# The opening of a fused retention and feed-forward kernel in another order on ScalarE, GpSimd, VectorE and the sync engine

## The chip, the core and the metric

The kernel runs on one core of a Trainium2 chip (trn2). A core has five engines, each with an instruction queue of its own that it works off in order: TensorE (PE) for matrix products, VectorE (DVE), ScalarE (ACT) and GpSimd (POOL) for element-wise work, and the sync engine (SP), which here only issues DMAs and passes semaphores on. The metric is the device time of one execution in microseconds (us), as the median of several runs.

## What is computed

Retention (a causal, decaying form of attention without softmax) over 4 batches, 8 heads, 576 positions and head size 64, then two feed-forward layers on 2304 tokens of width 512. Cut to what matters:

```python
def _attn_ref(q, k, v):
    scores = scale * np.matmul(q, k.transpose(0, 1, 3, 2))
    gamma = 1.0 - 2.0 ** (-5.0 - np.arange(H))
    Dmat = np.where(rel >= 0, gamma[:, None, None] ** rel[None], 0.0)
    return np.matmul(scores * Dmat[None], v)

def _moe_ref(x, w_in, w_out):              # 512 -> 2048 -> 512, ELU
    h = x @ w_in
    g = np.where(h > 0.0, h, np.exp(np.minimum(h, 0.0)) - 1.0)
    return g @ w_out

def _moe2_ref(x, w_gate, w_val, w_out):    # 512 -> 1536 -> 512, gated
    gate = 1.0 / (1.0 + np.exp(-(x @ w_gate)))
    return gate * (x @ w_val) @ w_out
```

## The kernel before

**Retention in steps.** The 2304 tokens are worked off in 18 steps of 128 tokens (class `Step`). A step has a chunk of q, k and v (1 MB, one DMA; the last step of each half of the batches has six smaller ones, `load`, L172 to L187). Its methods are: `scale` (POOL multiplies v by powers of gamma, L192), `scores` (32 small matmuls into the PSUM tile `ts`, L197), `causal` (VectorE masks them into `a`, L207), `sums` (32 matmuls of k and v into the low half of the PSUM tile `to`, L210), `states` (VectorE adds them to the running state in two operations, L228 or L230 and L232, then POOL scales it, L233), `inter` (state times q into the high half of `to`, L238), `outs` (masked scores times v, onto the same place, L250), `x_scaled` (VectorE takes the result out of `to`, L267; ScalarE rounds it to its high half, L272) and `x_low` (VectorE forms the low half, L275). `inter` and `outs` use different row tiles of TensorE, and `inter` of its first half is fenced off by a relay: a no-op on another engine waits for it, and `outs` waits for the no-op (`swept`, L248 and L259). For steps 0 to 5 (`RELAY = 6`) the no-op is in ScalarE's queue, after that in SP's.

**Feed-forward in pieces.** Every product runs as three passes over high and low halves (`mm3`, L85). The first pass over the weights is cut in pieces of 256 tokens (`FF` with `half`): pieces 0 and 1 take the tokens of steps 0 and 1 with the weights `weights[0]` and `weights[2]` (two column blocks of w_in), pieces 2 and 3 the tokens of steps 2 and 3, and so on. `ups` of a piece is 12 matmuls (L291), in the order high x high, high x low, low x high, then ScalarE's Relu and Exp (L306, L307), VectorE's combination (L310) and a split into g's high half (ScalarE, L82) and low half (POOL, L83). `downs` of a piece follow `LAG = 2` pieces later with `weights[1]` and `weights[3]` (blocks of w_out).

**Weights.** They are stored as 64-bit floats. `Weight.chain` (L114) turns one into two float32 halves in five stages: two conversions on ScalarE (L121, L122), two operations on VectorE (L124, L125), one (L128), one (L130), then the split, high half on ScalarE (L82) and low half on POOL (L83). It is a generator: each `next` (`stage()`) puts the next stage into the queues.

**The order is written by hand** (`manual_schedule`): each engine works in the order of the program text. `block(n)` (L429) interleaves step n and step n+1 on TensorE: inter(n), scores(n+1), outs(n), sums(n+1). The opening (L454 to L464) is warm-up matmuls (`WARM`), block(-1), block(0), block(1) without its next step, with four stages of `weights[0]` inside block(1), and then the loop over pieces s (L486). In it, before the change, `weights[2]` is converted during piece 0, `weights[1]` during pieces 1 and 2, `weights[3]` during pieces 2 and 3; steps 2 and 3 begin only behind the ups of piece 1 (L500 to L507), then block(2) and block(3); piece 2 follows with block(4) behind its ups, piece 3 with block(5). Loads of later steps are issued on SP at fixed blocks (`loads_at`): load 5 in block(0), 6 in block(1), and so on; load 8 is the one of six DMAs, in block(3).

Below, x(n) is the high half of the result of step n, and a name like sums(4) means that method of step 4.

Of the kernel before, what the change touches and what calls it, by code (L numbers as in the profile page):

```python
# [28 lines left out]
NSTEP = (B // 2) * NS  # L29
# [5 lines left out]
N0 = 256  # L35
AHEAD = 2
LATE = 4
RELAY = 6
SPARE = {3: 2, 8: 2, 4: 3, 9: 3, 14: 3}
LAG = 2  # L40
WARM = 24, 6, 2, 10
# [7 lines left out]
def retention_elu_glu(  # L49
# [13 lines left out]
    pe, act, dve, pool, sp = nc.tensor, nc.scalar, nc.vector, nc.gpsimd, nc.sync  # L63
# [27 lines left out]
    def warm_up(n):  # L91

        h = h_bank()
        for i in range(n):
            pe.matmul(h[:, :256], warm[:, :128], warm, start=True, stop=True)

    def after(ins, other):

        tc.add_manual_dep(ins.ins, other.ins.name, mybir.DependencyInfo(
            mybir.DependencyClass.Sync, mybir.DependencyReason.DATA), reason="row tiles")  # L100
        return ins
# [4 lines left out]
    class Weight:  # L106
# [3 lines left out]
        def load(self, raw=None):  # L110
            self.raw = rpool.tile([128, 2 * DM], I32, tag="raw", name="raw") if raw is None else raw
            sp.dma_start(out=self.raw, in_=self.src.bitcast(I32))
# [29 lines left out]
    W, weights, of_pass = {}, [], []  # L142
# [12 lines left out]
    class Step:  # L155
# [82 lines left out]
        def inter(self):  # L238

            for other in (1, 0):  # L240
                for p in range(NP):
                    for h in range(2):
                        X, r = h ^ other, slice(64 * h, 64 * h + 64)
                        if X or self.c:
                            ins = self.mm(self.o(h, X, p), self.st[X][r, p, :], self.q[r, p, HC * X : HC * X + HC], p == 0)
                if other:

                    self.swept = after((act if self.n < RELAY else sp).nop(), ins)  # L248

        def outs(self):  # L250

# [127 lines left out]
    with tc.manual_schedule():  # L379
# [19 lines left out]
        steps = [Step(n) for n in range(NSTEP)]  # L399
# [25 lines left out]
        loads_at = {}  # L425
        for m in range(5, NSTEP):
            loads_at.setdefault(m - 5 if m < 13 or m == 14 else m - 3 if m == 13 else m - 4, []).append(steps[m].load)

        def block(n, after_it=True, mid=(lambda: None,) * 2):  # L429

            after_it = after_it and n + 1 < NSTEP
            if n >= 0:
                steps[n].inter()
                mid[0]()
            if after_it:
                steps[n + 1].scores()
            if n >= 0:
                steps[n].outs()
            if after_it:
                steps[n + 1].sums(n < 0)  # L440
                steps[n + 1].causal()
            for load in loads_at.get(n, []):
                load()
            if n >= 0:
                steps[n].x_scaled()
            mid[1]()
            if after_it:
                steps[n + 1].states()
                if 2 <= n < NSTEP - 2:
                    steps[n + 2].scale()  # L450
            if n >= 0:
                steps[n].x_low()

        warm_up(WARM[0])  # L454
        steps[0].scale()
        block(-1)
        warm_up(WARM[1])
        steps[1].scale()
        block(0)
        warm_up(WARM[2])  # L460
        first = weights[0].chain()
        block(1, False, (lambda: (next(first), next(first)), lambda: (next(first), next(first))))
        next(first)
        warm_up(WARM[3])  # L464


# [4 lines left out]
                ff += [FF(kind, P if kind == "a" else P - FA // FP, g, f, fs) for g in range(NG) for f in fs]  # L471
                begins.append(len(ff))

        conv = {0: weights[2], 1: weights[1], 2: weights[3]}
        for P in range(len(passes) - 1):
            a, b, ws = begins[P], begins[P + 1], of_pass[P + 1]
            a += 6 * (P == 0) + LAG * (P == 1)
# [8 lines left out]
        for s in range(len(ff) + LAG):  # L486
            chain = conv[s].chain() if s in conv else None
            stage = lambda: next(chain) if chain is not None else None
            stage()
            if halves is not None:  # L490
                next(halves)
            halves = chain
            if LATE <= s < NSTEP - AHEAD:
                block(s + AHEAD)
            if s < len(ff):
                ff[s].ups(stage, s)
            else:
                stage()
                stage()
            if s == 1:  # L500
                steps[2].scale()
                steps[2].scores()
                steps[2].sums(True)
                steps[2].causal()
                steps[2].states()
                steps[3].scale()
                block(2)  # L507
            if 0 < s < LATE:
                block(s + AHEAD)
            for w in loads.get(s, []):  # L510
                w.load()
            if s >= LAG:
                ff[s - LAG].downs(stage)
            else:
                stage()
            if s == begins[1] + LAG - 1:
                ret.close()
                wpools.append(ctx.enter_context(tc.tile_pool(name="w2", bufs=4, side="right")))
                psum["acc"] = ctx.enter_context(tc.tile_pool(name="ps_acc", bufs=4, space=bass.MemoryType.PSUM))
                ps_t = ctx.enter_context(tc.tile_pool(name="ps_t", bufs=1, space=bass.MemoryType.PSUM))  # L520
                tv = ps_t.tile([128, 2, 512], F32, name="tv")
# [50 lines left out]
def build(nc, arrays):  # L572
    args = [
        nc.dram_tensor(f"in_{n}", a.shape, mybir.dt.from_np(a.dtype), kind="ExternalInput").ap()
        for n, a in arrays.items()
    ]
    args.append(nc.dram_tensor("out_0", (NT, DM), F32, kind="ExternalOutput").ap())
    with tile.TileContext(nc) as tc:
        retention_elu_glu(tc, *args)
# [12 lines left out]
```

## Time and profile before

| | |
|---|---|
| median of 3 runs | 943.82 us (940.94 to 944.57) |
| the profiled execution | 942.38 us |
| its span, first to last instruction | 940.6 us |
| TensorE busy in the span | 910.4 us (97%), 6418 matmuls |
| VectorE, ScalarE, GpSimd busy | 467.8, 365.2, 304.4 us |
| mean granted TensorE clock | 0.989 of full speed |

The profile's row of the granted clock in 40 slices of 23.5 us is 9 (90% or more) nearly everywhere; its second slice, 23.5 to 47 us, is 6. The idle time of TensorE lies almost wholly in the first three slices.

### The profile page before, as it was taken

The page shows a single profiled execution, that of the slowest core. Times are in us where ns is not written, and L with a number is a line of the kernel's source. Part 1 is how long each engine was busy: PE and PEld are TensorE (multiplying, and loading weights), DVE is VectorE, ACT ScalarE, POOL GpSimd, SP SyncE. Part 2 cuts the span into 40 slices and gives each one's busy share as a digit, 9 for nine tenths or more (in the row PEclk, how much of TensorE's full clock was granted, in tenths as well). Part 3 has the DMA queues.
Part 4 walks back from the last instruction along what each step waited for, and adds up shares of the span by engine and source line. Part 5 has one row for each costly group of instructions (what it writes and reads, how often), then busy time and mean ns, then how long its engine had stood idle before and what let it go on. Part 6 is the DMA issues. An engine that isn't in the chain of part 4 may idle for free.

```text
span 940.6 us, 15386 instructions
## 1 busy us (share of the span) xinstructions
PE 910.4 (97%) x6418; PEld 770.9 (82%) x6418; DVE 467.8 (50%) x756; ACT 365.2 (39%) x673; POOL 304.4 (32%) x264
## 2 busy tenths in 40 slices
PE   6589899999999999999999999999999999999998
PEld 5579898888888888888888888888888888888886
DVE  3476644555554655546786333534344455343223
ACT  2135465544554444544674333222223223222111
POOL 2364433333333332333664222222132222222111
PEclk9699999999999999999999999999999999999999
DMA  9365521111111011111211111111011011100113
GB/s 344 130 191 166 156 68 32 59 45 45 45 46 45 25 57 32 46 45 45 68 46 51 40 45 45 45 46 45 23 57 56 22 46 48 43 23 1 46 45 113
DMA packets 26998, 60.55 MB, mean 64 GB/s; under 512 B 6576, under 2 KB 7600, under 8 KB 26928
## 3 DMA queue, kind: packets, MB, share of 16 engines
q1 hardware_dynamic: 24864, 56.89, 19.1%
q10 hardware_dynamic: 2064, 2.67, 0.8%
q8 instruction: 50, 0.82, 0.4%
q14 instruction: 20, 0.16, 0.1%
HBM read 54.84 MB, written 4.72 MB: 63 GB/s over the span
## 4 chain that ended last, share of the span: by engine, by line
PE 94%; DVE 2%; ACT 1%; DMA 1%; POOL 1%; issue 1%; ACTq 0%; DVEq 0%; POOLq 0%
PE acc L87 12%; PE acc L88 12%; PE acc L89 12%; PE h L87 11%; PE h L89 11%; PE h L88 11%; PE tv L88 5%; PE tv L87 5%; PE tv L89 5%; PE to L195 4%; PE h L291 2%; PE ts L195 1%; DMA vt<-in_csmall 1%; DVE e L267 0%; POOL w L83 0%
## 5 line engine op out<-in xcount | busy, mean ns | idle before, releaser
L83 POOL TENSOR_TENSOR g<-e,g 128x512 fp32r<-128x512 f32 (+1 forms) x148 | 167.1, 1129 | 567.6 <-ACT g L82 528.0
L87 PE MATMUL h<-x,w 128*128 128x512 f32 (+1 forms) x520 | 192.5, 370 | 0.0
L88 PE MATMUL h<-x,w 128*128 128x512 f32 (+1 forms) x520 | 192.3, 370 | 0.0
L89 PE MATMUL h<-x,w 128*128 128x512 f32 (+1 forms) x520 | 192.3, 370 | 0.0
L82 ACT CAST g<-e 128x512 fp32r<-128x512 f32 (+1 forms) x148 | 82.5, 557 | 232.0 <-DVE e L318 154.8
L318 DVE TENSOR_TENSOR e<-e,tv 128x512 f32<-128x512 f32 (+1 forms) x60 | 38.0, 634 | 231.8 <-PE tv L89 231.8
L87 PE MATMUL acc<-g,w 128*128 128x512 f32 (+1 forms) x352 | 124.3, 353 | 0.6 <-ACT y L357 0.6
L88 PE MATMUL acc<-g,w 128*128 128x512 f32 (+1 forms) x352 | 123.8, 352 | 0.0
L89 PE MATMUL acc<-g,w 128*128 128x512 f32 (+1 forms) x352 | 123.8, 352 | 0.0
L310 DVE SCALAR_TENSOR_TENSOR e<-e,h 128x512 f32<-128x512 f32 (+1 forms) x88 | 51.9, 590 | 138.1 <-ACT e L307 137.5
L87 PEld LDWEIGHTS h<-x,w 128*128 128x128 f32 x520 | 97.9, 188 | 17.7
L89 PEld LDWEIGHTS h<-x,w 128*128 128x128 f32 x520 | 98.0, 188 | 17.6
L88 PEld LDWEIGHTS h<-x,w 128*128 128x128 f32 x520 | 97.9, 188 | 17.7
L83 POOL TENSOR_TENSOR w<-t,w 128x512 fp32r<-128x512 f32 x68 | 91.1, 1339 | 14.0 <-ACT w L82 13.7
L315 ACT ACTIVATE e<-h 128x512 f32<-128x512 f32 (+1 forms) x60 | 33.3, 555 | 154.3 <-PE h L89 147.7
L306 ACT ACTIVATE e<-h 128x512 f32<-128x512 f32 (+1 forms) x88 | 45.8, 520 | 114.1 <-PE h L89 96.8
L88 PE MATMUL tv<-x,w 128*128 128x512 f32 (+1 forms) x240 | 88.7, 370 | 0.0
L87 PE MATMUL tv<-x,w 128*128 128x512 f32 (+1 forms) x240 | 88.6, 369 | 0.0
L89 PE MATMUL tv<-x,w 128*128 128x512 f32 (+1 forms) x240 | 88.6, 369 | 0.0
L88 PE MATMUL acc<-w,g 128*128 128x512 f32 x216 | 84.6, 392 | 0.0
L87 PE MATMUL acc<-w,g 128*128 128x512 f32 x216 | 84.6, 392 | 0.0
L89 PE MATMUL acc<-w,g 128*128 128x512 f32 x216 | 84.4, 391 | 0.0
(72 smaller groups left out, 1345.7 us busy)
## 6 DMA issues: line engine op xcount, KB each, us to landing
in<-in_ain SPq DMA_DIRECT2D x12, 1024.0 KB, 5.5
raw<-in_w_in SPq DMA_DIRECT2D x16, 512.0 KB, 3.6
raw<-in_w_out SPq DMA_DIRECT2D x14, 512.0 KB, 3.5
raw<-in_w_gate SPq DMA_DIRECT2D x12, 512.0 KB, 3.5
raw<-in_w_val SPq DMA_DIRECT2D x12, 512.0 KB, 3.5
raw<-in_w_o SPq DMA_DIRECT2D x12, 512.0 KB, 3.5
y<-in_ain SPq DMA_DIRECT2D x4, 1024.0 KB, 7.5
out<-y SPq DMA_DIRECT2D x8, 256.0 KB, 2.1
```

The lines of the kernel that those rows point to most:

```text
L82: act.copy(hi, src)
L83: lo_engine.tensor_tensor(out=lo, in0=src, in1=hi.bitcast(F32), op=ALU.subtract)
L87: pe.matmul(out_, wh, xh, start=start, stop=False, skip_group_check=shared)
L88: pe.matmul(out_, wh, xl, start=False, stop=False, skip_group_check=shared)
L89: pe.matmul(out_, wl, xh, start=False, stop=stop, skip_group_check=shared)
L195: return pe.matmul(out_, w, x, start=start, stop=True, skip_group_check=True)
L291: pe.matmul(h, w[:, a, c[k]], x[:, b, k, t], start=i + k == 0, stop=i == 2 and k == KB - 1)
L306: act.activation(out=e, in_=h, func=AF.Relu, scale=-1.0)
L310: dve.scalar_tensor_tensor(out=e, in0=e, scalar=-1.0, in1=h, op0=ALU.add, op1=ALU.max)
L315: act.activation(out=e, in_=h, func=AF.Sigmoid)
L318: dve.tensor_tensor(out=e, in0=e, in1=v, op=ALU.mult)
```

## The change

The fixed helper `RELAY` goes: every relay is on SP. `block` loses its parameters for the opening, and the opening is written out. In it, ScalarE's conversions of `weights[0]` come first on ScalarE; step 1's states come ahead of step 0's x_scaled; the rest of `weights[0]` stands around x_low(0); `weights[2]` is converted whole ahead of piece 0; step 2 is scaled in the opening, and its scores, sums, causal and states stand behind piece 0 instead of piece 1. Six warm-up matmuls stand ahead of sums(0) instead of behind states(0). `weights[1]` is converted in one go between block(2) and block(3).

```diff
-RELAY = 6
@@ inter
-                    self.swept = after((act if self.n < RELAY else sp).nop(), ins)
+                    self.swept = after(sp.nop(), ins)
@@ the opening (block(-1), block(0), block(1) before)
+        w0, w2 = weights[0].chain(), weights[2].chain()
         warm_up(WARM[0])
         steps[0].scale()
-        block(-1)
+        steps[0].scores()
+        steps[0].causal()
         warm_up(WARM[1])
+        steps[0].sums(True)
+        steps[0].states()
         steps[1].scale()
-        block(0)
+        stages(w0, 1)
+        steps[0].inter()
+        steps[1].scores()
+        steps[0].outs()
+        steps[1].sums()
+        steps[1].causal()
+        steps[1].states()
+        for load in loads_at[0]:
+            load()
+        steps[0].x_scaled()
+        stages(w2, 1)
+        stages(w0, 1)
+        steps[0].x_low()
+        stages(w0, 2)
         warm_up(WARM[2])
-        first = weights[0].chain()
-        block(1, False, (lambda: (next(first), next(first)), lambda: (next(first), next(first))))
-        next(first)
+        steps[1].inter()
+        steps[1].outs()
+        for load in loads_at[1]:
+            load()
+        stages(w0, 1)
+        steps[1].x_scaled()
+        steps[1].x_low()
+        steps[2].scale()
+        stages(w2, 4)
         warm_up(WARM[3])
@@ the loop over pieces
-        conv = {0: weights[2], 1: weights[1], 2: weights[3]}
+        conv = {2: weights[3]}
@@ behind the ups of piece s
-            if s == 1:
-                steps[2].scale()
+            if s == 0:
                 steps[2].scores()
                 steps[2].sums(True)
                 steps[2].causal()
                 steps[2].states()
                 steps[3].scale()
+            if s == 1:
                 block(2)
+                for _ in weights[1].chain():
+                    pass
             if 0 < s < LATE:
                 block(s + AHEAD)
```

`stages(chain, n)` calls `next` n times. `block(n)` itself keeps its order: inter(n), scores(n+1), outs(n), sums(n+1), causal(n+1), loads, x_scaled(n), states(n+1), scale(n+2), x_low(n).

## Rows read from the trace of the kernel before

**Rows 1.** Stretches of the span: us, busy us (count) by engine, clock, DMA

```profile
10.00:16.90 6.90, 5.49 (x152) 4.75 (x152) 2.96 (x7) 1.90 (x2) 1.62 (x2) 0.75 1.04 394
...
24.13:28.40 4.27, 0.82 (x7) 0.83 (x8) 3.33 (x6) 2.84 (x6) 1.53 (x2) 1.00 0.90 333
28.40:40.95 12.55, 8.55 (x200) 7.47 (x198) 2.56 (x5) 1.21 (x3) 4.33 (x5) 0.50 0.02 7
...
60.88:940.60 879.72, 871.49 (x5517) 737.14 (x5516) 438.56 (x706) 349.15 (x643) 282.47 (x239) 1.00 0.17 54
```

**Rows 2.** TensorE's waits, whole span: line waited for: us, times, longest us

```profile
PE to L195 <- POOL in L192: 5.8, 2, 3.2
PE h L291 <- ACT w L82: 5.7, 2, 3.5
PE to L195 <- ACTq L248: 2.7, 2, 2.2
PE to L195 <- issue: 2.5, 2, 1.8
```

**Rows 3.** The chain that ended last: start us, us, what

```profile
36.41 1.86 PE to L195 x29
...
62.55 1.08 PE to L195 x29
...
65.32 1.63 PE h L291 x12
```

**Rows 4.** Timeline of VectorE: start us, us, line, tiles, [idle before <- releaser]

```profile
25.03 0.42 DVE L310 SCALAR_TENSOR_TENSOR e<-e,h 128x256 f32<-128x256 f32 x1
...
41.03 0.69 DVE L267 TENSOR_TENSOR e<-to,cq_sb 128x512 f32<-128x512 f32 x1 [1.01 <-PE to L195]
...
42.08 0.42 DVE L232 TENSOR_TENSOR y<-y,to 128x256 f32<-128x256 f32 x1
```

**Rows 5.** Timeline of TensorE, columns as in rows 4

```profile
16.97 0.27 PE L195 MATMUL to<-in,y 64*64 64x64 f32 x1 [1.24 <-DVE st L232]
...
23.39 0.74 PE L291 MATMUL h<-x,w 128*128 128x256 f32 x4 [0.16 <-POOL w L83]
...
42.56 0.37 PE L195 MATMUL to<-y,y 64*64 64x64 f32 x1 [1.61 <-DVE y L232]
...
47.89 1.96 PE L291 MATMUL h<-x,w 128*128 128x256 f32 x12 [1.48 <-ACT x L272]
...
53.45 0.69 PE L195 MATMUL to<-a,y 64*64 64x64 f32 x32 [2.24 <-ACTq L248]
```

**Rows 6.** Loads: SP's timeline, issues (KB, us to landing), steps' landings, instruction queue

```profile
6.08 0.34 SPq L112 DMA_DIRECT2D raw<-in_w_in  x1
...
raw<-in_w_in SPq DMA_DIRECT2D x1, 512.0 KB, 5.3
...
DMA to landing us min/median/max: 5.3/8.6/12.3
...
q8 instruction: 11, 0.18, 1.1%
```

**Rows 7.** Operations on weight tile t to 62 us: ns min/median/max, first to last

```profile
L124 DVE TENSOR_SCALAR t<-t x4: 428/772/1267, 18.5 to 49.5; 128x512 f32<-128x512 f32 x4
L125 DVE TENSOR_SCALAR t<-t x4: 426/428/1375, 19.0 to 50.8; 128x512 uint32<-128x512 uint32 x4
...
L83 POOL TENSOR_TENSOR w<-t,w x4: 1267/1368/1787, 22.0 to 58.6; 128x512 fp32r<-128x512 f32 x4
...
L128 DVE CUSTOM_DVE_ANT_0 t<-raw,t x2: 681/686/692, 19.9 to 24.2; 128x1024 uint16<-128x1024 uint16 x2
...
L130 DVE SCALAR_TENSOR_TENSOR t<-y,t x2: 1103/1104/1105, 48.5 to 56.7; 128x512 uint32<-128x512 uint32 x2
```

**Rows 8.** Load 8: SP's timeline and the durations of its issues (ns)

```profile
49.18 0.62 SPq L186 DMA_DIRECT2D y<-in_ain  x1
...
L184 SPq DMA_DIRECT2D y<-in_ain x4: 367/501/1689, 44.6 to 48.6; - x4
```

More of the change, by code (lines that the diff above doesn't have):

```diff
@@ L427, in retention_elu_glu, with block @@
             loads_at.setdefault(m - 5 if m < 13 or m == 14 else m - 3 if m == 13 else m - 4, []).append(steps[m].load)
[L429 to L435, printed above, removed]
+        def block(n):
+            more = n + 1 < NSTEP
+            steps[n].inter()
+            if more:
                 steps[n + 1].scores()
[L437 to L440, printed above, removed]
+            steps[n].outs()
+            if more:
+                steps[n + 1].sums()
                 steps[n + 1].causal()
@@ L443, in block, with stages @@
                 load()
[L444 to L447, printed above, removed]
+            steps[n].x_scaled()
+            if more:
                 steps[n + 1].states()
-                if 2 <= n < NSTEP - 2:
+                if n + 2 < NSTEP:
                     steps[n + 2].scale()
-            if n >= 0:
-                steps[n].x_low()
+            steps[n].x_low()
+        def stages(chain, n):
+            for _ in range(n):
+                next(chain)
+        w0, w2 = weights[0].chain(), weights[2].chain()
         warm_up(WARM[0])
         steps[0].scale()
-        block(-1)
+        steps[0].scores()
+        steps[0].causal()
         warm_up(WARM[1])
+        steps[0].sums(True)
+        steps[0].states()
         steps[1].scale()
-        block(0)
-        warm_up(WARM[2])
-        first = weights[0].chain()
-        block(1, False, (lambda: (next(first), next(first)), lambda: (next(first), next(first))))
-        next(first)
+        stages(w0, 1)
[12 more added lines that the diff above has]
+        stages(w0, 2)
+        warm_up(WARM[2])
+        steps[1].inter()
[7 more added lines that the diff above has]
+        stages(w2, 4)
         warm_up(WARM[3])
```

## The prediction

> **What bounds the kernel now.** I read the stretches of the span first [rows 1]. From 60.88 us to the end TensorE is busy 871.49 of 879.72 us, at the full clock: nothing that the change does to the opening makes that part shorter, it can only let it begin earlier. So the question is the date at which TensorE gets to the downs of piece 1, which begin at 60.88. Before that, TensorE's waits [rows 2] name who is late: POOL's scale of v (L192, 5.8 us in two waits, 3.2 and 2.6), ScalarE's high half of a weight (5.7 in two) and the relay on ScalarE's queue (2.7 in two, 2.2 the longer). [...] A block of one step (inter, scores, outs, sums) runs from 62.55 to 65.32, 2.77 us, at the full clock, and from 36.41 to about 41.0, 4.55 us, at half [rows 3].
>
> TensorE itself is not the bound of the opening; the queues of VectorE, POOL and ScalarE are, each in order. So I follow the chain through them and compare dates.
>
> **Part 1, step 0 and step 1.** Six warm-ups now stand ahead of sums(0) instead of behind it; sums(0) waits for scale(0) as before, so they cost nothing in either place but leave the gap behind it open. inter(0), scores(1), outs(0), sums(1) keep their dates. VectorE then does states(1) before x_scaled(0) instead of after; inter(1) writes the bank that x_scaled(0) reads, so it needs both in either order. The same 0.42+0.42+0.69 [rows 4]: inter(1) at 17.05, against 16.97 [rows 5]. Change: 0.
>
> **Part 2, weights[0].** Its bytes land at 6.08+5.3 = 11.4 [rows 6]; ScalarE's two conversions used to stand behind the relay of step 1, and now run at 11.4 to 12.8 while ScalarE has nothing else. VectorE's four operations cost 0.43+0.43+0.69+0.69 [rows 7], and x_low(0) 0.69 between them: from 17.0 to 19.9. ScalarE writes the high half by 20.55 (0.62), x(1) behind it by 21.2, POOL the low half by 21.85 (1.27). The ups of piece 0 begin at 21.2 and end at about 23.0; they ended at 23.39+0.74 = 24.13 [rows 5].
>
> **Part 3, weights[2] ahead of piece 0.** This is the new chain that sets the end. x_low(1) begins at 21.2 beside POOL's low half. The nearest row for an operation of VectorE with two inputs in SBUF that starts while POOL works is L130 with 1.10 in place of 0.69 [rows 7]: x_low(1) ends between 21.9 and 22.3, and I take 22.3. L124 then meets scale(2): between 0.43 and 1.27, I take 1.05, near the upper end, since POOL starts first. With 0.43, 0.69 and 0.69 VectorE is done at 25.2, ScalarE's high half at 25.8. Behind that in ScalarE's queue stand Relu and Exp of piece 0, although their bank is full at 23.0: 25.85 to 26.7; then L310 (0.42), causal(2), states(2) (two of 0.42) on VectorE [rows 4], causal taken as long as x_scaled's 0.69, and inter(2) starts at 28.75. Before it started at 36.41 [rows 3]. That is **7.7 us earlier**, of which 2.6 is the wait for scale(2), which POOL did only behind the low half of piece 1, and the rest the place of step 2 behind the ups of piece 1. The ups of piece 1 (high half at 25.8, POOL's low half by 27.1 to 27.6) end by 28.3 and fit ahead.
>
> [...]
>
> **Part 4, blocks 2 and 3.** Block 2: 28.75+2.77 = 31.5, at the full clock. x_scaled waits for the sums too (at 41.03 it is released by the last of them [rows 4]): 31.5 to 32.2, states(3) to 33.05, inter(3) at 33.1 against 42.56 [rows 5]: 9.5 earlier. Block 3 ends at 35.85.
> Now the price. All of weights[1] stands on VectorE between x_low(2) and causal(4), ahead of x_scaled(3), where it was done in pieces before and after. From 33.75: at least 0.43+0.43+0.69+0.69 = 2.24, at most 1.27+1.38+0.69+1.10 = 4.44 [rows 7]; scale(4) on POOL meets one of the first two, so I take 3.1, to 36.85. causal(4) 37.55, x_scaled(3) 38.2, x(3) on ScalarE 38.85: the ups of piece 2 begin at **38.9 against 47.89** [rows 5], 9.0 earlier, with bounds 9.9 and 7.7. Their fifth matmul waits for x_low(3) until 39.75: 8.8 remain.
>
> **Part 5, relays on SP.** Step 4's relay stood on ScalarE behind the high half of g of piece 2, which waits for VectorE: outs(4) at 53.45 after 2.24 us [rows 5]; step 5's lost 0.5 more [rows 2]. On SP the queue ahead is loads. Relay(0) stands behind the first nine loads, the last of them issued while scores(1) run. Relays 1 to 3 stand behind loads that wait for the outs of the step before, done by then. Relay(4) stands behind the six DMAs of load 8, which end at 49.18+0.62 = 49.8 [rows 8], 3.4 us after sums(4) of before (47.89-1.48 = 46.4 [rows 5]). Now sums(4) ends at 35.85, so SP is free at 39.3; the ups of piece 2 and the first half of inter(4) end at about 41.5. That is a cover of 2.2 us, so the wait goes whole: **2.75 us**. Sum so far 8.8+2.75 = 11.5.
>
> **What is late next.** Landings: of step loads issued in the first 13 us none took over 12.3 [rows 6], the last of these (step 4) left at 11.0 and is needed at 33; the low half of weights[1] is ready by 39 and needed at 43. From the ups of piece 2 on the work has the order of before, at the full clock, with TensorE the bound.
>
> **Part 6, the clock.** TensorE now idles from 35.85 to 38.9, 3.05 us. The rows nearest to that are the 3.2 us wait for scale(0) and the 3.5 us wait for a weight [rows 2]; behind both the clock fell, after the first for (1-0.75)x2x6.90 = 3.45 us [rows 1], after the second for much longer, with TensorE idle again and again. After 38.9 it is not idle, so I take the short fall: half of 3.45, **1.7 us lost**. Bounds: 0, and some 5 if blocks 2 and 3 run at half too (1.8 each, partly behind VectorE).
> [...]
>
> **Sum.** 11.5 - 1.7 = 9.8 us. The profiled execution took 942.4 (span 940.6 and 1.8 around it); 942.4 - 9.8 = 932.6. The median of the runs, 943.8, is 1.4 above that execution, so I forecast **934.0**.
>
> **The rivals.**
> (a) The clock holds through the hole at 36: 11.5, so 932.3. For it: 2.24 us of idle at 53.45 left it full. Against it: the two longer waits.
> (b) The clock falls earlier, at about 25 to 28, as before: blocks 2 and 3 at 4.55 in place of 2.77, of which VectorE's chain hides little: -9.8+1.8+1.8 and another short fall give -4.5, so 939.3, or 937 with one of them. For it: TensorE is busy little more than half the time from 19.8 to 28.7. Against: in before, it fell only after 0.82 of 4.27.
> (c) SP is the new bound: load 8's six issues stretch over the 2.2 us of cover, because its DMAs queue behind others. One such issue took 1.69 against 0.5 [rows 8]; two slow ones use the cover up, all six slow give back 6x1.19-2.2 = 4.9, four of them 2.6: about 936.6. The same price if the relays gain nothing because another wait stands in the place of ScalarE's (VectorE's L310 and causal): 934.0+2.75 = 936.8. So the change would not do what it says.
> (d) Slower: code. Twice in the span TensorE's small matmuls wait with no releaser in the trace ("issue" [rows 2]), 0.7 and 1.8 us. Code comes in pieces; from 28 to 92 us there were eleven on the instruction queue [rows 6]. If a denser opening makes each of them late by as much, that is 11x0.7 = 8 to 11x1.8 = 20 us; from 1.3 us a piece on the kernel is slower by over 0.5%, at the upper end 954. Against it: TensorE runs just as dense from 60.88 on [rows 1], and waits so only twice.
>
> **How the numbers follow.** Forecast 0.43 (own range 932 to 936), a 0.22, b 0.17, c 0.10, d 0.04, and 0.04 for nothing gained for a reason not seen here. Low end: a with the lower price of weights[1] and a run lower than the median, 930. High end: b, 939. The measurement tells about 0.5% (4.7 us, so 939.1) from no change. Faster: forecast, a, c and most of b, 0.84; same 0.12; slower 0.04.
>
> **What would show it.** inter(2) near 29, inter(3) near 33, ups of piece 2 near 39, no wait of outs(4); a new wait of TensorE for ScalarE's x near 36 to 39, released by x_scaled(3) behind weights[1]'s L130; clock below 1 for one short stretch after it. Wrong if inter(2) starts after 31 (part 3), if that new wait is over 5 us (part 4), if outs(4) waits for SP (part 5), or if TensorE has over 6 us of "issue".

## The result, and the profile after

| | before | after |
|---|---|---|
| median (lowest to highest) | 942.68 us (940.94 to 944.57, 4 runs) | 931.64 us (931.25 to 932.52, 4 runs) |
| the profiled execution | 942.38 us | 931.67 us |
| its span | 940.6 us | 929.9 us |
| mean granted TensorE clock | 0.989 | 0.991 |

The ratio is 0.9884 (0.986 to 0.9907): 11.0 us, or 1.2%, faster. The forecast was 934.0 with a range of 930 to 939. Lines of the changed kernel have a number lower by one than before up to the opening, since the line of `RELAY` is gone: L195 of before is L194.

First the stretches, cut at the end of sums(4), the ups of piece 2, outs(4) and the downs of piece 1 (span, then busy us and count of TensorE, its weight loads, VectorE, ScalarE and GpSimd, granted clock, DMA share, GB/s):

```profile
36.33:39.32 2.99, 0.01 (x3) 0.00 (x1) 2.92 (x7) 1.29 (x3) 1.18 (x1) 1.00 0.99 200
39.32:43.88 4.56, 4.56 (x66) 4.13 (x69) 3.70 (x6) 2.14 (x5) 2.22 (x3) 0.63 0.32 87
43.88:50.51 6.63, 6.63 (x224) 6.36 (x216) 4.68 (x8) 2.49 (x6) 4.42 (x4) 1.00 0.56 163
50.51:929.90 879.39, 871.56 (x5522) 737.16 (x5516) 438.65 (x707) 349.36 (x643) 283.63 (x240) 1.00 0.17 54
```

From the downs of piece 1 to the end it takes 879.4 us, as it did before [rows 1]. The whole gain lies ahead of that date, 50.51 against about 60.8. Next the new hole: 2.99 us without TensorE, in which VectorE is busy throughout. Behind it come the ups of piece 2, mostly at half the clock (0.63 in the mean of the stretch).

TensorE's waits by what ended them (us in total, times, longest):

```profile
PE h L290 <- ACT x L271: 4.2, 2, 3.0
PE to L194 <- issue: 2.2, 2, 1.3
PE to L194 <- POOL in L191: 1.9, 1, 1.9
PE to L194 <- DVE y L231: 1.6, 1, 1.6
```

Of the rows of before [rows 2], the wait for ScalarE's half of a weight (5.7) and the one for the relay on ScalarE's queue (2.7) are gone; the wait for POOL's scale is down from 5.8 to 1.9. What is new is ScalarE's x, 4.2, of which 2.98 is the hole. Up to the downs of piece 1 the waits sum to 22.0 us before and 12.3 after; TensorE's busy time there went from 38.8 to 38.1. So nearly all of the gain is waiting that is no longer there.

The dates in TensorE's timeline (start, duration, line, operation, tiles, and in brackets the idle time before and its releaser):

```profile
17.58 0.27 PE L194 MATMUL to<-in,y 64*64 64x64 f32 x1 [1.19 <-DVE e L266]
...
21.59 0.73 PE L290 MATMUL h<-x,w 128*128 128x256 f32 x4 [1.20 <-ACT x L271]
...
29.22 0.27 PE L194 MATMUL to<-in,y 64*64 64x64 f32 x1 [0.46 <-DVE st L231]
...
33.38 0.27 PE L194 MATMUL to<-y,y 64*64 64x64 f32 x1 [1.61 <-DVE y L231]
...
39.32 2.81 PE L290 MATMUL h<-x,w 128*128 128x256 f32 x12 [2.98 <-ACT x L271]
...
43.88 0.52 PE L194 MATMUL to<-a,y 64*64 64x64 f32 x22
```

| date of | before | predicted | after |
|---|---|---|---|
| inter(1) | 16.97 | 17.05 | 17.58 |
| ups of piece 0 | 22.02 | 21.2 | 21.59 |
| inter(2) | 36.41 | 28.75 | 29.22 |
| inter(3) | 42.56 | 33.1 | 33.38 |
| ups of piece 2 | 47.89 | 38.9 | 39.32 |
| downs of piece 1 | 60.81 | (9.8 earlier) | 50.51 (10.3 earlier) |

The row of outs(4) at 43.88 (22 of its 32 matmuls) has no wait in brackets, where before had 2.24 [rows 5]; nor have those of the other ten.

### The profile page after: what moved, and what is told of

It is laid out like the page before. It is cut to its first block, busy times and chain, and to the rows that moved or that the text cites. A ratio compares the mean times of both kernels' runs of the same rounds, so it can differ in the third digit from the quotient of the medians.

```text
span 929.9 us, 15387 instructions
## 1 busy us (share of the span) xinstructions
PE 909.7 (98%) x6418; PEld 770.0 (83%) x6418; DVE 468.5 (50%) x756; ACT 365.5 (39%) x673; POOL 304.2 (33%) x264
## 4 chain that ended last, share of the span: by engine, by line
PE 95%; DVE 3%; DMA 1%; issue 1%; ACT 0%; ACTq 0%; POOL 0%; DVEq 0%; POOLq 0%
PE acc L86 12%; PE acc L87 12%; PE acc L88 12%; PE h L86 12%; PE h L88 12%; PE h L87 12%; PE tv L87 5%; PE tv L86 5%; PE tv L88 5%; PE to L194 4%; PE h L290 3%; PE ts L194 1%; DMA vt<-in_csmall 1%; DVE e L266 0%; DVE x L274 0%
## 5 line engine op out<-in xcount | busy, mean ns | idle before, releaser
L317 DVE TENSOR_TENSOR e<-e,tv 128x512 f32<-128x512 f32 (+1 forms) x60 | 38.1, 635 | 231.4 <-PE tv L88 231.4
L309 DVE SCALAR_TENSOR_TENSOR e<-e,h 128x512 f32<-128x512 f32 (+1 forms) x88 | 51.9, 590 | 137.0 <-ACT e L306 136.5
```

The lines of the kernel that those rows point to most:

```text
L309: dve.scalar_tensor_tensor(out=e, in0=e, scalar=-1.0, in1=h, op0=ALU.add, op1=ALU.max)
L317: dve.tensor_tensor(out=e, in0=e, in1=v, op=ALU.mult)
```

## The experiments

The kernel before ran beside each set, with medians of 943.24, 942.47 and 942.32 us. relays_alone, act_relays, step2_late and w1_spread stood beside the first of these, fill_hole, after_again, w1_after and exp_first beside the second, the rest beside the third. The dates of a profiled execution are best counted from its ups of piece 0, since the opening up to there runs faster or slower with the clock from one execution to the next (the last section has the dates). In before, relays_alone and scale2_early the work ahead of that date differs too. Counted so, in us:

| kernel | median | ups of piece 0 at | to inter(2) | to ups of piece 2 | to downs of piece 1 |
|---|---|---|---|---|---|
| before | 942.68 | 22.02 | 14.39 | 25.87 | 38.79 |
| relays_alone | 939.18 | 21.32 | 14.41 | 24.02 | 34.67 |
| after | 931.64 | 21.59 | 7.63 | 17.73 | 28.92 |
| after_again | 931.16 | 20.76 | 7.34 | 17.44 | 28.64 |
| act_relays | 933.90 | 21.87 | 7.63 | 19.37 | 31.23 |
| step2_late | 934.40 | 20.72 | 10.74 | 20.83 | 32.03 |
| scale2_late | 933.24 (1) | 19.42 | 11.38 | 21.47 | 32.40 |
| scale2_early | 931.25 (1) | 22.18 | 6.77 | 16.87 | 28.06 |
| fill_hole | 929.14 | 21.14 | 7.63 | 17.73 | 27.45 |
| w1_spread | 932.08 | 20.73 | 8.68 | 17.08 | 28.01 |
| w1_after | 932.67 | 21.91 | 7.64 | 16.03 | 29.29 |
| exp_first | 931.18 | 20.45 | 7.10 | 18.39 | 29.48 |
| w1_two | 929.50 | 20.79 | 7.64 | 16.72 | 27.92 |
| warm6_back | 933.29 (1) | 20.68 | 7.64 | 18.99 | 30.20 |

(1): one execution.

**relays_alone: only the relays, in the kernel before.**

```diff
-RELAY = 6
-                    self.swept = after((act if self.n < RELAY else sp).nop(), ins)
+                    self.swept = after(sp.nop(), ins)
```

> The kernel before with every relay on SP and nothing else. Theory (the prediction's part 5): the two waits behind ScalarE's relay, 2.24 and 0.51 us, go whole: 942.7 - 2.75 = 939.9, and the downs of piece 1 begin 2.7 us earlier than 60.8, at 58.1. Rival: another wait stands in their place. In the kernel before, VectorE is busy with weights[3] and L310 until 53.3, so causal(5) and the L130 of weights[3] come at most 0.8 us earlier, and its low half on POOL, ready at 59.9 before, at 59.1: then the downs of piece 1 begin at 59.2 or later, TensorE has a new wait of about 1 us for POOL, and the time is 941.1.

Measured: 939.18 us (938.21 to 940.46), ratio 0.9955 (0.994 to 0.997), 4.1 us less than before. TensorE's timeline has small waits where the two of ScalarE's queue had been:

```profile
45.34 1.95 PE L290 MATMUL h<-x,w 128*128 128x256 f32 x12 [1.46 <-ACT x L271]
...
52.84 0.27 PE L194 MATMUL to<-in,y 64*64 64x64 f32 x1 [0.18 <-DVE st L231]
...
55.37 0.69 PE L194 MATMUL to<-in 64*64 64x64 f32 x32 [0.45 <-POOL in L191]
```

From the ups of piece 2 to the downs of piece 1 (55.99) it is 10.65 us, against 12.92 before: 2.27 gained, although new waits of 0.18 and 0.45 came in (for VectorE's states and POOL's scale). A second gain stands in part 2 of the prediction, among the dates of weights[0], and not with the relays: the ups of piece 0 begin 0.70 earlier (21.32), since ScalarE's conversions of weights[0] stand behind no relay any more and begin at 16.62 instead of 17.79. Between the two, from the ups of piece 0 to those of piece 2, it takes another 1.85 less; I put that down to the clock, whose stretch at half behind 28.2 lasted 10.2 us in this execution and 17.1 in that of before. A fall at 103.31, for 3.41 us, took back some 1.7 (half of it, an estimate). So the relays alone are worth 3.0 us by the rows (2.27 and 0.70) and 4.1 by the medians, against 2.75 for the two waits, and the old order gives little of it back.

**act_relays: the changed kernel with the relays of steps 0 to 5 on ScalarE again.**

```diff
-                    self.swept = after(sp.nop(), ins)
+                    self.swept = after((act if self.n < 6 else sp).nop(), ins)
```

> The changed kernel with the relays of steps 0 to 5 back on ScalarE. Theory: in the new order a relay on ScalarE costs more than the one wait of before. Step 3's stands behind the high half of weights[1] (ends at 38.07 in the changed kernel), so outs(3) waits from 34.8 to 38.1, x_scaled(3) from 37.9 to 39.4: 1.4 us on the way to the ups of piece 2; steps 4 and 5 stand behind the high halves of g, 0.3 and 1.0 us. Sum 2.7: 931.6 + 2.7 = 934.3. Rival: in the new order the relays are hidden by VectorE's conversion of weights[1] and it makes no difference, 931.6. Third: the prediction's own 2.75 at the places of before (2.24 at outs(4), 0.5 at outs(5), none at outs(3)).

Measured: 933.9 us (932.59 to 935.41), ratio 0.99 (0.9882 to 0.9919); the change as it is has 931.64. In the timeline of TensorE the relay is waited for three times:

```profile
37.79 1.13 PE L194 MATMUL to<-a,y 64*64 64x64 f32 x32 [2.52 <-ACTq L247]
41.24 2.93 PE L290 MATMUL h<-x,w 128*128 128x256 f32 x12 [1.46 <-ACT x L271]
...
45.73 0.69 PE L194 MATMUL to<-a,y 64*64 64x64 f32 x32 [0.21 <-ACTq L247]
...
52.00 0.69 PE L194 MATMUL to<-a,in 64*64 64x64 f32 x32 [0.50 <-ACTq L247]
```

The price, 2.3 us by the downs of piece 1, is near the 2.7 that were expected, but its place is not the one that part 5 of the prediction names. outs(4), which lost 2.24 in before, loses only 0.21. The long wait, 2.52, is at outs(3). Step 3's relay now stands on ScalarE behind the high half of weights[1], and that conversion waits for VectorE's four operations, as ScalarE's timeline of this run shows:

```profile
37.72 0.62 ACT L81 CAST w<-t 128x512 fp32r<-128x512 f32 x1 [3.08 <-DVE t L129]
```

So in the new order it is mostly weights[1], converted in one go, that a relay on ScalarE has to wait for.

**step2_late: the changed kernel with step 2's scores, sums, causal, states and step 3's scale behind piece 1 again.**

```diff
-            if s == 0:
+            if s == 1:
                 steps[2].scores()
                 steps[2].sums(True)
                 steps[2].causal()
                 steps[2].states()
                 steps[3].scale()
-            if s == 1:
                 block(2)
```

> The changed kernel with step 2's scores, sums, causal and states behind the ups of piece 1 again, as before; scale(2) stays early. Theory (part 3): the place of step 2 is worth more than the wait for scale(2): causal(2) now stands behind the L309 of piece 1 (29.7 to 30.1), states(2) end at 31.7, inter(2) begins at 31.75 in place of 29.2, and all behind it is 2.5 us later: 934.1. Rival: the conversion of weights[1] on VectorE, or another queue behind it, sets the date anyway, and the earlier place gives nothing: 931.6. Rival 2: the place is all of the 7.2 us that inter(2) gained: 938.8.

Measured: 934.4 us (933.74 to 935.6), ratio 0.9907 (0.989 to 0.9923). Timeline of TensorE:

```profile
31.46 0.27 PE L194 MATMUL to<-in,y 64*64 64x64 f32 x1 [1.43 <-DVE st L231]
```

Counted from the ups of piece 0, inter(2) is 3.1 us later than in the changed kernel, and so is all that follows. The reason is VectorE: causal(2) starts at 29.93, behind the combination (L309) of piece 1 at 29.60, and that waited 2.70 us for ScalarE's Exp:

```profile
29.60 0.42 DVE L309 SCALAR_TENSOR_TENSOR e<-e,h 128x256 f32<-128x256 f32 x1 [2.70 <-ACT e L306]
29.93 0.68 DVE L206 TENSOR_TENSOR a<-ts,tri 128x512 f32<-128x512 f32 x1
```

Not all of the 3.1 is the place. In this execution the clock stood at half from 22.4 to 29.2, and the ups of piece 1, on whose end that Exp waits, took 2.92 us; in the changed kernel they took 2.11 with a wait in between. So some 0.8 is the clock's, by an estimate from these rows, and the medians differ by 2.8. The place of step 2 ahead of piece 1 is a part of the gain by itself, 2 to 3 us.

**scale2_late: the changed kernel with scale(2) behind the ups of piece 0, in front of scores(2); one execution.**

```diff
         steps[1].x_low()
-        steps[2].scale()
         stages(w2, 4)
...
             if s == 0:
+                steps[2].scale()
                 steps[2].scores()
```

> The changed kernel with scale(2) behind POOL's work for piece 0, as late as its scores: one look. Theory (part 3): POOL does it only after the low halves of weights[2] and of g of piece 0, so at 29.0 to 30.1; sums(2) wait for it, and behind them on TensorE stand the ups of piece 1: inter(2) at 32.5 in place of 29.2, 3.3 us, 934.5. Rival: scale(2)'s place costs what it was read as in the kernel before, one wait of 2.6, and inter(2) comes at 31.8.

Measured: 933.24 us. Timeline of TensorE:

```profile
27.06 0.99 PE L194 MATMUL to<-in 64*64 64x64 f32 x32 [4.50 <-POOL in L191]
```

That is sums(2), after a wait of 4.50 us: POOL reaches scale(2) at 25.96 only, since it works in order and stands at the low halves of weights[2] and of g. GpSimd's timeline:

```profile
25.96 1.05 POOL L191 TENSOR_TENSOR in<-in,vt 128x512 f32<-128x512 f32 x1
```

The ups of piece 1 queue behind sums(2), from 27.98 to 30.87. Counted from the ups of piece 0, inter(2) is 3.7 us later than in the changed kernel. Some 1.2 of that is the clock, which fell at 27.28, behind that wait (an estimate: sums(2) and the ups took 0.99 and 2.89 us, and 0.69 and 1.95 are what such rows take at full clock). That shows less in the time, which is 1.6 above the change's profiled execution, since the opening ran 2.2 us earlier here, at the full clock up to 27.28.

**scale2_early: scale(2) still further ahead, in front of inter(1); one execution.**

```diff
+        steps[2].scale()
         warm_up(WARM[2])
         steps[1].inter()
...
         steps[1].x_low()
-        steps[2].scale()
         stages(w2, 4)
```

> The changed kernel with scale(2) ahead of the low half of weights[0] on POOL, where it can start at 17.6: one look at which operations of VectorE get long. [...]

Measured: 931.25 us. It is read in four operations of VectorE and the ones of GpSimd beside them. In VectorE's timeline of the changed kernel,

```profile
17.93 0.43 DVE L124 TENSOR_SCALAR t<-t 128x512 uint32<-128x512 uint32 x1
...
21.57 1.27 DVE L274 TENSOR_TENSOR x<-e,x 128x512 fp32r<-128x512 f32 x1 [0.69 <-ACT x L271]
22.76 1.27 DVE L123 TENSOR_SCALAR t<-t 128x512 f32<-128x512 f32 x1
```

are the second operation on weights[0] (L124), x_low(1) and the first operation on weights[2] (L123). The last two stand beside POOL's low half of weights[0] and scale(2), in GpSimd's timeline of the same kernel:

```profile
21.02 1.27 POOL L82 TENSOR_TENSOR w<-t,w 128x512 fp32r<-128x512 f32 x1 [3.40 <-ACT w L81]
22.25 1.50 POOL L191 TENSOR_TENSOR in<-in,vt 128x512 f32<-128x512 f32 x1
```

With scale(2) moved, L123 of weights[2] is short, and L124 of weights[0], now beside scale(2), is long (VectorE, then GpSimd, in scale2_early):

```profile
17.79 1.16 DVE L124 TENSOR_SCALAR t<-t 128x512 uint32<-128x512 uint32 x1
...
23.35 0.41 DVE L123 TENSOR_SCALAR t<-t 128x512 f32<-128x512 f32 x1
```
```profile
17.43 1.23 POOL L191 TENSOR_TENSOR in<-in,vt 128x512 f32<-128x512 f32 x1
```

L124 was 0.43 in the change and is 1.16; L123 was 1.27 and is 0.41. If the long time belonged to L123 or to its date, it would have stayed at 1.27: here the cost went with POOL's operation to its new place. In weights[0] it delays the ups of piece 0 by about as much as it then saves up to inter(2), and the time stays.

**fill_hole: the changed kernel with 24 warm-up matmuls in the new hole; after_again: the changed kernel beside it.**

```diff
             if 0 < s < LATE:
                 block(s + AHEAD)
+            if s == 1:
+                warm_up(24)
```

> The changed kernel with 24 warm-up matmuls in TensorE's 2.98 us wait ahead of the ups of piece 2. Theory (part 6): the wait lets the clock fall at 40.07 for 3.4 us, and the warm-ups, some 2.5 us at the full clock, keep it up; the stretch from 39.3 to 43.9 (ups of piece 2, inter(4), scores(5)), 4.6 us at half, becomes 3.5, so about 1.1 is gained: 930.5. Rival: TensorE then waits for others; the low half of weights[3] is ready at 50.3 in the changed kernel, 0.2 before the downs of piece 1 begin, so only about 0.2 comes through and the rest turns into a wait ahead of those downs: 931.4.

> The changed kernel itself, as the comparison for the three beside it: 931.6, within the 930.2 to 933.0 that single executions of it spread over. In the profile the clock should fall once in the opening for each long wait of TensorE (ahead of the ups of piece 2, and early), at dates that differ by some us from execution to execution.

Measured: fill_hole 929.14 us (927.73 to 930.38), ratio 0.9861 (0.9844 to 0.9878); after_again 931.16 us (928.88 to 932.35), ratio 0.9876 (0.9859 to 0.9893). Timeline of fill_hole:

```profile
35.82 2.79 PE L94 MATMUL h<-y 128*128 128x256 bf16 x24
38.87 1.95 PE L290 MATMUL h<-x,w 128*128 128x256 f32 x12 [0.26 <-ACT x L271]
...
41.97 0.52 PE L194 MATMUL to<-a,y 64*64 64x64 f32 x22
```

The warm-ups take the time in which TensorE would have waited; 0.26 of the wait is left. The clock stays at 1.00, and the ups of piece 2 take 1.95 instead of 2.81. From them to the downs of piece 1 (48.59) it takes 9.72 us instead of 11.19 (11.20 in after_again). So the fall of the clock behind the hole costs **1.5 us** in these executions. By the medians the two kernels are 2.0 apart, with overlapping intervals; that is not all the clock's, since further back TensorE's waits with no releaser sum to 2.03 us in this execution of fill_hole and to 3.10 in that of after_again (2.74 in after). The rival's wait for weights[3] did not come: its low half was ready at 48.39, counted from the ups of piece 0 1.5 earlier than in the change, since the work ahead of it moved too. fill_hole is the fastest of the kernels tried, below both kernels, though the step to the change itself is 0.2% and its runs don't separate it well.

**w1_spread: the first stages of weights[1], three operations of VectorE among them, in the opening behind those of weights[2], the rest behind block(3).**

```diff
-        stages(w2, 4)
+        stages(w2, 3)
+        w1 = weights[1].chain()
+        stages(w1, 3)
+        stages(w2, 1)
...
-                for _ in weights[1].chain():
-                    pass
             if 0 < s < LATE:
                 block(s + AHEAD)
+            if s == 1:
+                stages(w1, 2)
```

> The changed kernel with weights[1] in two parts: its ScalarE stage and three of its four VectorE operations in the opening, right behind weights[2]'s VectorE operations, the last one and the split behind block(3). Theory (part 4): weights[1] on VectorE between x_low(2) and causal(4) makes TensorE's 2.98 us wait ahead of the ups of piece 2. Without it x_scaled(3) waits only for sums(4), which end at 36.3, and x(3) is there at 37.75: the ups begin 1.55 us earlier, at 37.8, the wait shrinks to 1.4 us, and with it the clock's fall at 40.07 may go, which cost about 1.3: 930.1 without that, 928.8 with it. Rival: the conversion only moves the delay: three operations of VectorE ahead of the L309 of piece 0 push causal(2) and inter(2) by as much as they take away: 931.6.

Measured: 932.08 us (930.24 to 933.15), ratio 0.9878 (0.9859 to 0.9898): no gain over the change. The wait ahead of the ups of piece 2 is halved (1.46) and the clock didn't fall there in the profiled execution. But VectorE had no room in the opening. Its timeline:

```profile
26.00 1.64 DVE L127 CUSTOM_DVE_ANT_0 t<-y,t 128x1024 uint16<-128x1024 uint16 x1
27.57 0.41 DVE L309 SCALAR_TENSOR_TENSOR e<-e,h 128x256 f32<-128x256 f32 x1
```

L127, 0.69 elsewhere, met POOL's low half of weights[2] (25.81 to 27.10) and took 1.64; the combination of piece 0 and all of step 2 stand behind it, and inter(2) starts after a wait of 1.52 (0.46 in the changed kernel). Later it waits 0.47, 0.45 and 0.23. Counted from the ups of piece 0, inter(2) is 1.05 later than in the change, the ups of piece 2 0.65 earlier and the downs of piece 1 0.9 earlier, in an execution that was itself faster than the median of its kernel. The gain that was expected went to the operation that met POOL and to the waits behind.

**w1_after: the whole of weights[1] behind block(3).**

```diff
-                for _ in weights[1].chain():
-                    pass
             if 0 < s < LATE:
                 block(s + AHEAD)
+            if s == 1:
+                for _ in weights[1].chain():
+                    pass
```

> The changed kernel with weights[1] whole behind block(3) instead of ahead of it. Theory: the ups of piece 2 begin 1.55 us earlier (at 37.8, bound by x_scaled(3) behind sums(4)), but the low half of weights[1] is now late for the downs of piece 0: VectorE's four operations from 38.4 to 41.6, ScalarE to 42.2, POOL to 43.5 or later, so the downs begin at 43.5 to 44 in place of 45.0, and weights[3] stands 3 us further back, its low half at 51 to 52 for downs of piece 1 that began at 50.5. Sum between 1 earlier and 1 later: 931.6. Rival: the place ahead of block(3) costs its full 3 us and nothing is late behind it: 928.6.

Measured: 932.67 us (931.55 to 933.0), ratio 0.9896 (0.9881 to 0.9911). Timeline of TensorE:

```profile
37.94 1.95 PE L290 MATMUL h<-x,w 128*128 128x256 f32 x12 [1.46 <-ACT x L271]
...
42.81 0.39 PE L86 MATMUL acc<-g,w 128*128 128x256 f32 x1 [0.62 <-ACT w L81]
...
44.17 0.39 PE L88 MATMUL acc<-g,w 128*128 128x256 f32 x1 [0.86 <-POOL w L82]
```

Counted from the ups of piece 0, the ups of piece 2 come 1.7 earlier, and the downs of piece 0 then wait for the same weight, first for its high half, then for its low half. The clock fell at 44.45, and the downs of piece 1 are 0.4 later than in the change. The weight must be ready by its first use, and moving the wait did not shorten it here: 1.46, 0.62 and 0.86 make 2.94, against 2.98 in the change.

**exp_first: the split of weights[2] behind Relu and Exp of piece 0, and weights[1] in three portions (opening, behind states(2), behind block(3)).**

```diff
-        stages(w2, 4)
+        stages(w2, 3)
+        w1 = weights[1].chain()
+        stages(w1, 1)
...
+            if s == 0:
+                calls = iter((None, None, w2))
+                stage = lambda: [next(c) for c in [next(calls, None)] if c is not None]
...
                 steps[2].states()
+                stages(w1, 2)
                 steps[3].scale()
...
-                for _ in weights[1].chain():
-                    pass
             if 0 < s < LATE:
                 block(s + AHEAD)
+            if s == 1:
+                stages(w1, 2)
```

> The changed kernel with three moves: the split of weights[2] stands behind Relu and Exp of piece 0 on ScalarE; weights[1]'s ScalarE stage in the opening and two of its VectorE stages behind states(2); the rest of weights[1] behind block(3). Theory: nothing stands on VectorE ahead of L309 of piece 0 (in w1_spread 1.1 us of weights[1] did), inter(2) is then bound by the ups of piece 1, 28.8 in place of 29.2, the ups of piece 2 begin at 37.4 in place of 39.3, and the clock holds: 931.6 - 1.9 = 929.7, or less by 1 with the clock. Rival: three operations of VectorE beside POOL's states(2) and scale(3) hold each other up, sums(3) wait for scale(3), and 1 to 2 us are given back: 931.

Measured: 931.18 us (929.55 to 933.33), ratio 0.9883 (0.9865 to 0.9901), the same as after_again. Counted from the ups of piece 0, inter(2) came 0.5 earlier than in the change, as meant, but the operations of weights[1] behind it and scale(3) on POOL held each other up (L127 0.98 in place of 0.69, L191 1.49 in place of 1.05). Timeline of TensorE:

```profile
29.96 0.69 PE L194 MATMUL to<-y 64*64 64x64 f32 x32 [0.34 <-POOL y L191]
...
36.84 0.56 PE L194 MATMUL to<-y 64*64 64x64 f32 x20 [0.72 <-issue]
38.84 2.82 PE L290 MATMUL h<-x,w 128*128 128x256 f32 x12 [1.43 <-ACT x L271]
```

sums(3) waits for that scale, sums(4) waits 0.72 with no releaser in the trace, and the clock fell at 32.57 already and again at 39.4. This execution is also the slowest of the kernel's five, with one more fall, at 97.4, far behind the opening. By the ups of piece 2 the lead had become 0.7 of delay.

**w1_two: ScalarE's stage and VectorE's first two operations of weights[1] in the opening, the rest where the change has it.**

```diff
-        stages(w2, 4)
+        stages(w2, 3)
+        w1 = weights[1].chain()
+        stages(w1, 2)
+        stages(w2, 1)
...
-                for _ in weights[1].chain():
-                    pass
+                stages(w1, 3)
```

> The changed kernel with ScalarE's stage of weights[1] and only the first two of its VectorE operations (L123, L124 of the changed file) in the opening, behind weights[2]'s, where VectorE idles 1.4 us; the other two and the split stay between block(2) and block(3). Theory: w1_spread lost what it gained because a third operation met POOL there (1.64 us in place of 0.69) and pushed L309 of piece 0; two operations, 0.43 each, end before it. Then 2 us of VectorE (L123 and L124 took 0.84 and 1.16 between the blocks) leave the way to the ups of piece 2, TensorE's wait shrinks from 2.98 to about 1, and the clock holds: 931.2 - 2.0 - 1.5 = 927.7; without the clock 929.2. Rival: the two meet POOL as well and inter(2) is later by 0.5 to 1: 930 to 931.

Measured: 929.5 us (928.44 to 930.48), ratio 0.9865 (0.9849 to 0.9882). Timeline of VectorE, then of TensorE:

```profile
33.05 1.10 DVE L127 CUSTOM_DVE_ANT_0 t<-y,t 128x1024 uint16<-128x1024 uint16 x1
34.18 1.42 DVE L129 SCALAR_TENSOR_TENSOR t<-y,t 128x512 uint32<-128x512 uint32 x1
```
```profile
37.51 2.43 PE L290 MATMUL h<-x,w 128*128 128x256 f32 x12 [1.70 <-ACT x L271]
```

The two operations of 0.42 fit into VectorE's idle time of the opening and nothing behind them was late: inter(2) starts at 28.43. The wait ahead of the ups of piece 2 shrinks from 2.98 to 1.70, by 1.3 and not by the 2.0 that the two operations took in the change, since the other two now met POOL's work and took 1.10 and 1.42 instead of 0.69 each. The clock still fell, behind this shorter wait (38.75, for 3.41). Of all placements of weights[1] this is the only one that keeps what it gains: 1.0 us at the downs of piece 1. Its median is below that of the change by 2.1 us (1.7 against after_again), with intervals that overlap.

**warm6_back: the six warm-ups behind states(0) again; one execution.**

```diff
-        warm_up(WARM[1])
         steps[0].sums(True)
         steps[0].states()
+        warm_up(WARM[1])
```

> The changed kernel with the six warm-ups back behind states(0): one look. Theory: the gap of 2 us ahead of sums(0) becomes 3, the one of 1 us behind it closes, and the first fall of the clock, 6.8 us long in the changed kernel and 3.4 in the one before, is 3.4 again; sums(1) end 0.5 earlier, and inter(2), bound by VectorE, moves by no more than that: 931. Rival: the length of that fall differs from execution to execution with the same kernel, and the place of six warm-ups does nothing.

Measured: 933.29 us. The clock's first fall is not held off by them; stretches at half clock (columns as above):

```profile
10.66:14.07 3.41, 3.41 (x75) 2.88 (x76) 0.73 (x3) 1.23 (x2) 1.62 (x2) 0.50 1.02 390
27.72:31.14 3.42, 2.96 (x78) 2.82 (x78) 0.93 (x3) 1.21 (x3) 2.71 (x4) 0.50 0.12 41
```

A second fall came at 27.72, ahead of block(2), and block(2) ran at half: inter(3) stands 13.06 us behind the ups of piece 0, against 11.79 in the change. This is rival (b) of the prediction, in an order almost the same. That the six warm-ups cause or prevent anything of it isn't shown: one execution can't tell them from the spread that is told at the end.

## Why the prediction was right

**Part 1 (0.5 late).** The order came out as told: x_scaled(0) releases inter(1). But the clock fell at 9.35, for 6.83 us, instead of at 11.34 for 3.41, and everything from sums(0) to sums(1) ran at half. This was no term of the sum.

```profile
9.35:16.18 6.83, 5.54 (x146) 5.05 (x146) 1.67 (x4) 1.23 (x2) 1.86 (x3) 0.50 1.04 392
23.01:26.42 3.41, 3.41 (x68) 3.19 (x72) 2.83 (x4) 0.44 (x1) 0.74 (x1) 0.50 1.05 391
```

The second stretch made the last eight matmuls of the ups of piece 0 take 2.00 instead of 1.2, and it is hidden: what follows waits for ScalarE's Exp, whose predecessors on VectorE end at 25.94.

**Parts 2 and 3 (7.7 predicted, 7.2 measured).** At the ups of piece 0 it is 0.4 late, which comes from part 1. Counted from inter(1) they come at 5.05 us before, at 4.42 with nothing but the relays moved (relays_alone) and at 4.01 in the change, so more than half of what was gained there is the relay's. Behind them the way to inter(2) shrank from 14.39 to 7.63 us, by 6.8. Some 0.9 of this is the clock, by an estimate from rows: in before it stood at half from 28.40 on [rows 1], where the last four matmuls of the ups of piece 1 and sums(2) took 1.23 and 1.13 us in place of 0.74 and 0.69. The prediction priced none of it here. Undoing step 2's place costs 3.1 (step2_late), undoing scale(2)'s 3.7 (scale2_late), with 0.8 and 1.2 of the clock in them. That both are needed is shown. Whether the two add isn't, though they sum to 6.8: a late scale(2) in the new order holds up the ups of piece 1 as well, and the clock is in both; nor was the earlier conversion of weights[2] undone by itself. The sizes that were off are those of two operations beside POOL's: x_low(1) took 1.27 (predicted 1.10) beside the low half of weights[0] (POOL from 21.02 for 1.27), and the first operation of weights[2] 1.27 (1.05) beside scale(2) (from 22.25 for 1.50). With scale(2) moved away the latter took 0.41 (scale2_early). The row of that operation in before went up to 1.27 [rows 7], and the prediction should have taken that for both. At inter(2) the lateness is 0.5 all the same, because behind the high half of weights[2] 0.3 came back: the sum adds up whole durations, and in the rows an operation starts before the one ahead of it has ended (26.50 to 29.17; causal(2) starts at 27.70, while the combination of piece 0, from 27.36, takes 0.42).

**Part 4 (9.0 predicted, 8.6 measured).** weights[1] held VectorE from 33.85 to causal(4) at 37.33, 3.5 us against 3.1, within its bounds. Again operations beside POOL's make the difference, as VectorE's timeline shows; one of the first two was priced as longer, and both were, 0.84 and 1.16 in place of 0.43, beside POOL's two (33.41 to 35.60):

```profile
33.85 0.84 DVE L123 TENSOR_SCALAR t<-t 128x512 f32<-128x512 f32 x1
34.72 1.16 DVE L124 TENSOR_SCALAR t<-t 128x512 uint32<-128x512 uint32 x1
```

The wait for ScalarE's x ahead of the ups of piece 2 is there, 2.98 against a forecast hole of 3.05. The 0.2 that was taken off for x_low(3) was no loss: in before, too, the ups of piece 2 took 1.96 [rows 5] where those of the next piece take 1.60.

**Part 5 (2.75 predicted, some 3.2 measured).** At full clock, in fill_hole, the way from the ups of piece 2 to the downs of piece 1 takes 9.72, and 12.92 before: 3.2. Of that, 2.75 is the two waits. For the rest of the 3.2 I have only a reading: where outs(4) no longer waits, TensorE's rows of fill_hole show its first seven matmuls in between those of scores(5) and its last three in between those of sums(5) (22 of 32 are in the row at 41.97; before, all 32 stood in one row). That was not tried by itself. SP was free in time, as predicted: its last issue of load 8 began at 38.66 and took 0.62, and the relay was passed after 42. The step of the prediction that is wrong here is the place, as act_relays shows: in the new order it is outs(3) that would have waited.

**Part 6 (1.7 predicted, 1.5 measured).** The clock fell at 40.07, behind the hole, for 3.41 us; fill_hole, which fills the hole and does nothing else, has no such fall, while all six profiled executions with the hole at its 2.98 us have one; from the ups of piece 2 to the downs of piece 1 those six take 10.93 to 11.21 us, fill_hole 9.72.

**The sum.** Up to the downs of piece 1: 8.6 + 3.2 - 1.5 = 10.3 (predicted 9.8). That this is so near is in part luck, since errors of both signs cancel: the dates came 0.4 late, and the 0.2 for x_low(3), the 0.4 of part 5 and the 0.2 of part 6 went the other way. Of the remaining 0.4 of the profiled executions' 10.7, TensorE's waits with no releaser make 0.35: 2.74 between 83 and 96 us in after, 3.09 between 93 and 107 before. The 1.4 us that the forecast added, because the median of three runs lay above the profiled execution, was spread of three runs: the three later medians of before are 943.2, 942.5 and 942.3, and the profiled 942.4 was typical. Without it the forecast would have been 932.6.

**The rivals.** (a), the clock holds: not in the profiled executions of after and after_again. It may in others: two of the five executions of after_again took 928.9 and 929.3 with a mean clock of 0.998, the other three 931.2 to 932.4 with 0.991 to 0.996. (b), the clock falls ahead of blocks 2 and 3: not in after, where the early falls ended ahead of block(2), but in warm6_back (in front of block 2) and in exp_first (in block 3). So it was a real case, at 1.3 us where it was seen. (c), SP: no wait for SP in any kernel that has the relays there. (d), code: the waits with no releaser sum to between 2.0 and 3.9 us in the profiled executions with the new opening and to 3.09 before, so the denser opening adds nothing that shows.

## What to carry to other kernels

Where an order is written by hand, price a moved operation by the queue it joins on every engine: here one conversion placed on VectorE decided which relay on ScalarE would stall (2.52 us at outs(3) in act_relays). The hole ahead of a dense stretch cost more than its length here: behind 2.98 us of it the clock fell, for another 1.5 us (11.19 against 9.72), and matmuls of no use in the hole gave that part back. Moving work out of the wait was worth less than the wait: of four other placements of the same conversion three gave the gain back, to GpSimd's operations beside it or to the weight's first use.

## What the runs showed of the hardware

The dates and lengths at which the clock falls differ from execution to execution of the same code (after stood at half from 9.35 on, after_again at 1.00 up to 12.6). In ten of the profiled executions the work up to inter(1) is that of the change, but for one relay. The first stretch at half clock began there at 9.35 to 12.68 and lasted 6.83 us in some and 3.41 in others; in one, scale2_late, there was none before 27.28. inter(1) came at 15.41 in that one and between 16.4 and 17.9 in the others. I take this for a part of the 2 to 3 us by which runs of one kernel differ. What sets these dates no run shows.

No length of a wait divides the cases in which the clock fell from those in which it held: it fell behind a wait of 1.70 us in w1_two and of 2.98 in after, and stayed full behind 1.46 in w1_spread and 2.24 in before [rows 1, 5]. In after it fell at 23.01 too, behind waits of 1.20 and 0.57.

Beside GpSimd's work an operation got longer that the prediction had not priced so, the custom one on 16-bit integers (0.69 alone, 1.10 in w1_two, 1.64 in w1_spread). And GpSimd's own scale took 1.49 instead of 1.05 where VectorE had begun first (scale(3) behind L127 in exp_first, scale(4) in w1_two).
